# Attention's first casts of k on VectorE, a later clear of zero rows, and expert 6's row loads ahead of its store

## The chip, the cores and the metric

One NeuronCore of a Trainium2 chip runs the whole program in one launch. The metric is the device time of one execution in microseconds; runs of a kernel are told by their median.

## The reference, cut to what matters

```python
scores = scale * np.matmul(q, k.transpose(0, 1, 3, 2))        # 4 x 12 heads, 448 x 64, causal
attn = softmax(masked scores)
x = np.matmul(attn, v) -> 1792 rows of 768
e_idx = np.argmax(x @ w_gate, axis=1)                          # one expert of 8 for each row
for e in range(E):
    ye = np.maximum(x[mask] @ w1[e], 0.0) @ w2[e]              # mask = e_idx == e
    out[mask] = gate_w[mask, None] * eom[mask, e, None] * ye
h = out @ w_in                                                 # last stage, 768 -> 2048 -> 768
return (h - np.tanh(h)) @ w_out
```

## The kernel before, in words

All numbers that TensorE multiplies are kept as two f16 planes, a cast and the rest that the cast left, so almost every load is followed by a cast and a subtraction on some engine. Each engine has one queue of instructions in program order, and SP's queue issues nearly all DMAs.

**Attention** (lines 240 to 760) runs over 24 units of two heads; four heads (two units) share one load, numbered z. For z = 0 the loads come head by head (L285 for q and k, L287 for v), and `kq_part(h)` makes the planes of head h: ScalarE casts q into `qa` (L290), k is cast into `kh` by VectorE for heads 0 and 1 (L292) and by ScalarE for heads 2 and 3 (L294), VectorE subtracts to make `kl` (L295), GpSimd subtracts to make the second half of `qa` (L296). Heads 0 and 1 are done ahead of the loop over units, heads 2 and 3 as parts at the places `START = ((0, 1), (0, 2), ...)` inside unit 0, and v's planes follow (L300 on VectorE, L269 and L270 on GpSimd). For z = 1 and later the casts and rests go to GpSimd and ScalarE (L316, L318, L334), and small DMAs carry the results into `kh`, `qa` and `kl` (L332, L333, L335, L336). The lower 64 partitions of `kl` are filled by those DMAs; the upper 64 must be zero, and GpSimd clears them once for each of the two `kl` tiles: `kls[1]` at L305, between heads 1 and 2 of z = 0, and `kls[0]` at L675, in unit 2. Within a unit, m runs over score tiles: TensorE multiplies (L360, L361), VectorE takes the maximum (L367), ScalarE the exponential (L375).

**Experts.** Each expert has a first slot of 128 rows (expert 0 has two) and up to four extra slots under `If`s on the number of its rows. A slot is two products on TensorE with a relu between (`hh` on ScalarE L171, `hl` on VectorE L172). At the end of a slot `yo` is stored to `ys_d` by SP (L923). In a first slot the next expert's weights are made into planes: `hi(z)` on ScalarE (L115), `lo(z)` on VectorE (L123), and `lo(3)` stands behind the store in the program. For expert 6 `lo(3)` also loads a flag on SP (L1253) and issues six loads of 128 x 768 rows from `ys_d` (`prep0`, L1071) into free parts of the raw weight tiles, for the last stage. In the extra slots `conv_fill` turns three units of the last stage's weights each: SP loads the words into `cu` (L990), VectorE unpacks them into `cc` (L980, L983, L986), ScalarE and VectorE or GpSimd make planes in `co` (L115, L123, L117, L131), and SP stores them to `wb_d` (L1007).

**The last stage** makes planes of the rows in `ys_d`, then 80 tiles of product, activation and product (L1379, L1387 to L1408, L1430) and an indirect store.

What sets the order is the order of the code; each DMA that reads or writes what an earlier DMA touched waits on that DMA's semaphore. In `slot` the end of a slot reads:

```python
        st = nc.sync.dma_start(out=ys_d[ds(r0, 128)], in_=yo).ins      # L923
        ...
        lo(3)
        fill(4)
```

Of the kernel before, what the change touches and what calls it, by code (L numbers as in the profile page):

```python
# [17 lines left out]
AF = mybir.ActivationFunctionType  # L18
# [8 lines left out]
E, F1 = 8, 1024  # L27
# [32 lines left out]
def build(ctx: ExitStack, tc: tile.TileContext, kq0, kq, v, wg, wo, w1, w2, wf, out):  # L60
    nc = tc.nc
# [95 lines left out]
    def slot_xT(src, tag, pool):  # L157
        planes_T(src.rearrange("p (k x n) -> p k x n", k=KD, x=2), xTs[tag][:, 0], xTs[tag][:, 1], pool)
# [22 lines left out]
    with ExitStack() as actx:  # L181
# [68 lines left out]
        def load_32(z):  # L250
            b, hh = divmod(z, 3)
            t32, v32 = views(z)
            nc.sync.dma_start(out=t32, in_=kq[b, hh])
            nc.sync.dma_start(out=v32, in_=v[b, hh])

        kls = [ld.tile([128, HU, S], F16, tag=f"kl{n}", name=f"kl_{n}", bufs=1) for n in range(2)]

        def load_unit(z):
            b, hh = divmod(z, 3)
            t32, v32 = views(z)  # L260
            t = []

            def t_new():
                t.extend((ld.tile([128, HU, S], F16, tag="qa", name=f"qa_{z}"), ld.tile([128, HU, S], F16, tag="kh", name=f"kh_{z}"),
                          kls[z % 2]))

            def v0_planes(hs):
                src = t[3][:, hs, 0, :]
                nc.gpsimd.tensor_scalar(out=t[4][:, 0, hs], in0=src, scalar1=1.0, scalar2=1.0, op0=ALU.mult, op1=ALU.mult)  # L269
                nc.gpsimd.tensor_tensor(out=t[4][:, 1, hs], in0=src, in1=t[4][:, 0, hs], op=ALU.subtract)  # L270

            def v1_new():
                v1 = ld.tile([CP, HU, NCH, D + 1], F32, tag="v1", name=f"v1_{z}", bufs=3)
                nc.gpsimd.memset(v1[:, :, :, D : D + 1], 1.0)
                t.append(v1)
                t.append(ld.tile([CP, 2, HU, D + 1], F16, tag="v0", name=f"v0_{z}", bufs=3))

            if z == 0:
                t_new()
                v1_new()  # L280
                qa, kh, kl = t[0:3]
                f32 = raw2.rearrange("p a b -> p (a b)")[:, 0 : 2 * NS].rearrange("p (h x n) -> p h x n", h=HU, x=2)
                k32, q32 = f32[:, :, 0], f32[:, :, 1]
                for h in range(HU):
                    nc.sync.dma_start(out=f32[:, h : h + 1], in_=kq0[:, h : h + 1])  # L285
                    if h % 2:
                        nc.sync.dma_start(out=v32[:, h - 1 : h + 1], in_=v[b, hh, :, h - 1 : h + 1])  # L287

                def kq_part(h):
                    nc.scalar.activation(out=qa[:, h], in_=q32[:, h], func=AF.Copy)  # L290
                    if h < 2:
                        nc.vector.tensor_copy(out=kh[:, h], in_=k32[:, h])  # L292
                    else:
                        nc.scalar.activation(out=kh[:, h], in_=k32[:, h], func=AF.Copy)  # L294
                    nc.vector.tensor_tensor(out=kl[:, h], in0=k32[:, h], in1=kh[:, h], op=ALU.subtract)  # L295
                    nc.gpsimd.tensor_tensor(out=qa[64:128, h], in0=q32[64:128, h], in1=qa[64:128, h], op=ALU.subtract)  # L296

                def v_part(h):
                    hs = slice(h, h + 2)
                    nc.vector.tensor_scalar(out=t[3][:, hs, :, 0:D], in0=v32[:, hs], scalar1=XS, scalar2=None, op0=ALU.mult)  # L300
                    v0_planes(hs)

                kq_part(0)
                kq_part(1)
                nc.gpsimd.memset(kls[1][64:128], 0.0)  # L305
                return t, (lambda: kq_part(2), lambda: kq_part(3), lambda: v_part(0), lambda: v_part(2))
            if z != 2:
                load_32(z)
            tmp = []

            def cast(y, eng):
                hs = slice(2 * y, 2 * y + 2)
                if y == 0:
                    tmp.extend(ld.tile([128, HU, S], F16, tag=tag, name=f"{tag}_{z}", bufs=1) for tag in ("t16", "lo"))
                if eng == "a":
                    nc.scalar.activation(out=tmp[0][:, hs], in_=t32[:, hs], func=AF.Copy)  # L316
                else:
                    nc.gpsimd.tensor_scalar(out=tmp[0][:, hs], in0=t32[:, hs], scalar1=1.0, scalar2=1.0, op0=ALU.mult, op1=ALU.mult)  # L318

            def rest(y):  # L320
                hs = slice(2 * y, 2 * y + 2)
                if y == 0:
                    t_new()
                    v1_new()
                if z == 1:
                    cast(y, "pa"[y])
                t16, lo = tmp
                qa, kh, kl = t[0:3]
                if z == 1 or y == 0:
                    cs = hs if z == 1 else slice(0, HU)  # L330
                    for p0 in (0, 64):
                        nc.sync.dma_start(out=kh[p0 : p0 + 64, cs], in_=t16[0:64, cs])  # L332
                    nc.sync.dma_start(out=qa[0:64, cs], in_=t16[64:128, cs])  # L333
                nc.gpsimd.tensor_tensor(out=lo[:, hs], in0=t32[:, hs], in1=t16[:, hs], op=ALU.subtract)  # L334
                nc.sync.dma_start(out=qa[64:128, hs], in_=lo[64:128, hs])  # L335
                nc.sync.dma_start(out=kl[0:64, hs], in_=lo[0:64, hs])  # L336
                nc.gpsimd.tensor_scalar(out=t[3][:, hs, :, 0:D], in0=v32[:, hs], scalar1=XS, scalar2=1.0, op0=ALU.mult, op1=ALU.mult)
                v0_planes(hs)

            return t, rest, cast  # L340
# [286 lines left out]
        def fill0(n):  # L627
            for _ in range(n):
                next(s0, None)

        loads = {0: load_unit(0)}
        nc.sync.dma_start(out=wgf[:, :, 0:E], in_=wg)
        nc.sync.dma_start(out=wgf[:, :, E:], in_=wo)
# [18 lines left out]
        for u in range(NU + 5):  # L652
# [18 lines left out]
            for m in range(6):  # L671
                if (u, m) == (0, 3):
                    load_32(2)
                if (u, m) == (2, 0):
                    nc.gpsimd.memset(kls[0][64:128], 0.0)  # L675
                for x, part in zip(START, loads[0][1]):
# [202 lines left out]
    def slot(e, i, w, tag, fill=None, trans=(), then=(), late=False, mid=None):  # L879
        hi, lo = fill if isinstance(fill, tuple) else (lambda z: None, lambda z: None)  # L880
        fill = fill if late else (lambda z: None)
        hh = mt.tile([128, KF1, 128], F16, tag="hh", name=f"hh_{nc.get_next_instruction_name()}", bufs=1)
        hl = mt.tile([128, KF1, 128], F16, tag="hl", name=f"hl_{nc.get_next_instruction_name()}", bufs=1)
        static = isinstance(i, int) and i <= FB[e]
        yo = mt.tile([128, DM], F32, tag="ys" if static else "yo", name=f"yo_{nc.get_next_instruction_name()}", bufs=1)
        trans = list(trans)

        def rows_T(z):
            if trans:
                src, dst = trans.pop(0)  # L890
                slot_xT(rows[src], dst, mp_t)
                if z < len(then):
                    then[z]()

        def out_z(z, py):
            nc.scalar.activation(out=yo[:, z * 384 : (z + 1) * 384], in_=py[:, 0:384], func=AF.Copy)
            fill(2 + z)

        hi(0)
        slot_relu(0, slot_mm1(e, i, 0, w, tag), hh, hl)  # L900
        hi(1)
        lo(0)
        fill(0)
        slot_relu(1, slot_mm1(e, i, 1, w, tag), hh, hl)
        rows_T(0)
        fill(1)
        hi(2)
        lo(1)
        py = slot_mm2(e, i, 0, w, hh, hl, mid)
        hi(3)  # L910
        out_z(0, py)
        rows_T(1)
        lo(2)
        py = slot_mm2(e, i, 1, w, hh, hl)
        hi(4)
        out_z(1, py)
        j = i - FB[e]
        if isinstance(j, int) and j == 0:
            cstr[0] = nc.values_load(cst0[0:1, e : e + 1], engines=(SP,), min_val=0, max_val=NT)
            r0 = cstr[0]  # L920
        else:
            r0 = nc.snap(cstr[0] + j * 128, engines=(SP,), min_val=0, max_val=NT)
        st = nc.sync.dma_start(out=ys_d[ds(r0, 128)], in_=yo).ins  # L923
        if isinstance(i, int):
            tc.declare_no_dep(st, group=f"ys{e}", reason="blocks of one expert have rows of their own in ys_d")
            tc.add_to_no_dep_group(f"ys{e}", st)
            if j == 0 and e:
                after(st, ystores[e - 1])
            ystores.setdefault(e, []).append(st.name)
        lo(3)  # L930
        fill(4)

    cstr = [None]
# [607 lines left out]
```

## Time and profile before

| what | value |
|---|---|
| runs | 998.45, 1002.32, 1003.99 us, median 1002.32 us |
| profiled execution | 1004.1 us, its span 1002.4 us, granted clock 0.994 |
| TensorE busy | 957.7 us (96%) |
| VectorE busy | 787.3 us (79%) |
| ScalarE busy | 615.1 us (61%) |
| GpSimd busy | 471.1 us (47%) |
| DMA | 166.36 MB, mean 166 GB/s |

The page shows the shares over the whole span; the parts of the kernel have different limits, so a stretch is read by its own busy times, its DMA share and the waits of TensorE in it. Times in rows count from the start of the span.

### The profile page before, as it was taken

To read this page: it belongs to the slowest core of one execution; us is meant where nothing else is said; L and a number is where in the kernel's file an instruction comes from. 1 tells how busy PE (TensorE), PEld (TensorE's weight loads), DVE (VectorE), ACT (ScalarE), POOL (GpSimd) and SP (SyncE) were. 2 spreads that over 40 slices of the span, in tenths; PEclk is the share of its full clock that TensorE was granted. 3 is DMA by queue.
4 is the path that set the end of the run, shared out by engine and by line. 5 is a ranking of instruction groups with operands and counts; after the bars stand their busy time and mean duration, and the time that the engine had idled before them with its cause. 6 is when DMAs were issued, how large, how long until landed. Compare 5 with 4: busy or idle time off the path is not lost. (4 is left out here: it accounts for less than half of the span.)

```text
span 1002.4 us, 24099 instructions
## 1 busy us (share of the span) xinstructions
PE 957.7 (96%) x9177; PEld 714.8 (71%) x9177; DVE 787.3 (79%) x1740; ACT 615.1 (61%) x1176; POOL 471.1 (47%) x536
## 2 busy tenths in 40 slices
PE   4999999998999999899999899999999999999996
PEld 3998989986787878667776556666666666667764
DVE  6788888977879598687888999986988788786640
ACT  5898988773645475563346896665655555565530
POOL 8568887872201020201345797564534444453321
PEclk9999999999999999999999999999999999999999
DMA  9787786576799998879877430010000000000000
GB/s 244 204 236 209 226 227 181 162 250 226 261 362 327 383 340 307 327 285 346 320 271 274 169 153 17 32 33 9 32 25 33 17 25 17 9 17 17 16 25 24
DMA packets 59831, 166.36 MB, mean 166 GB/s; under 512 B 7920, under 2 KB 21872, under 8 KB 56608
## 3 DMA queue, kind: packets, MB, share of 16 engines
q1 hardware_dynamic: 55120, 144.68, 43.1%
q0 software_dynamic: 4560, 19.80, 5.7%
q8 instruction: 80, 1.31, 0.5%
q14 instruction: 71, 0.58, 0.2%
HBM read 122.21 MB, written 29.62 MB: 151 GB/s over the span
## 5 line engine op out<-in xcount | busy, mean ns | idle before, releaser
L1430 PE MATMUL fo<-wo,g 128*128 128x384 f16 x1344 | 228.2, 326 | 0.0
L1379 PEld LDWEIGHTS <-raw 128*128 128x128 f16 x1440 | 140.6, 98 | 83.2 <-issue 4.8
L1430 PEld LDWEIGHTS <-g 128*128 128x128 f16 x1344 | 131.1, 98 | 83.9
L1389 POOL TENSOR_TENSOR V<-cu,cc 128x384 f32<-128x384 f32 (+1 forms) x80 | 78.6, 983 | 186.2 <-ACT cu L1388 185.2
L164 PEld LDWEIGHTS <-w 128*128 128x128 f16 x2592 | 145.8, 98 | 7.9 <-issue 6.8
L1379 PE MATMUL fh<-cu,raw 128*128 128x384 f16 (+1 forms) x864 | 131.5, 308 | 2.2 <-DVE cc L1387 2.2
L375 ACT ACTIVATE P<-s,nb 112x112 f32<-112x112 f32 (+1 forms) x192 | 91.2, 508 | 20.7 <-DVE nb L367 18.7
L115 ACT ACTIVATE w<-raw 128x768 f16<-128x768 f32 (+2 forms) x106 | 90.8, 907 | 17.9 <-DMA raw<-w 15.3
L123 DVE SCALAR_TENSOR_TENSOR w<-raw,w 128x768 f16<-128x768 f32 (+1 forms) x99 | 99.7, 1067 | 0.2 <-ACT w L115 0.2
L861 POOL DMA_INDIRECT xg<-xs_d,idx x22 | 26.8, 1218 | 155.2 <-DMA xg<-xs_d,idx 23.5
L1388 ACT ACTIVATE cu<-cc 128x384 f32<-128x384 f32 (+1 forms) x80 | 40.0, 501 | 92.9 <-DVE cc L1387 92.9
L367 DVE CUSTOM_DVE_ANT_0 s<-s,maskw 112x112 f32<-112x112 f32 (+1 forms) x192 | 86.2, 454 | 12.8 <-PE s L361 8.6
L1387 DVE TENSOR_TENSOR cc<-fh,co 128x384 f32<-128x384 f32 (+1 forms) x80 | 42.0, 524 | 63.2 <-PE fh L1379 50.2
L1392 POOL TENSOR_TENSOR X<-cc,X 128x384 f32<-128x384 f32 (+1 forms) x80 | 88.4, 1105 | 4.1 <-ACT X L1391 0.6
L424 PE MATMUL o<-v,PT 112*112 112x65 f32 x576 | 84.5, 270 | 0.0
L1399 DVE SCALAR_TENSOR_TENSOR V<-cu,V 128x384 f32<-128x384 f32 (+1 forms) x80 | 82.3, 1028 | 0.2
L1407 DVE TENSOR_TENSOR V<-V,co 128x384 f32<-128x384 f32 (+1 forms) x64 | 77.8, 1215 | 0.0
L1408 ACT ACTIVATE g<-V 128x384 f16<-128x384 f32 (+1 forms) x80 | 40.0, 500 | 46.2 <-DVE V L1407 46.1
L424 PEld LDWEIGHTS o<-v,PT 112*112 112x112 f32 x576 | 68.4, 179 | 0.0
L1379 PE MATMUL fh<-yh,raw 128*128 128x384 f16 x384 | 67.6, 326 | 0.7 <-DVE cc L1387 0.7
L394 PE MATMUL t<-ident,P 112*112 112x112 f32 x480 | 67.4, 263 | 0.0
L360 PE MATMUL s<-kh,qa 128*112 128x112 f16 (+1 forms) x192 | 53.7, 300 | 13.3 <-POOL qa L296 7.2
(677 smaller groups left out, 2093.9 us busy)
## 6 DMA issues: line engine op xcount, KB each, us to landing
raw<-w SPq DMA_DIRECT2D x48, 512.0 KB, 7.3
raw<-w SPq DMA_DIRECT2D x64, 384.0 KB, 9.4
cu<-wf SPq DMA_DIRECT2D x22, 1024.0 KB, 7.8
wb_d<-co SPq DMA_DIRECT2D x22, 512.0 KB, 7.4
raw<-kq SPq DMA_DIRECT2D x11, 896.0 KB, 7.1
raw<-wb_d SPq DMA_DIRECT2D x8, 768.0 KB, 4.5
xs_d<-xq SPq DMA_DIRECT2D x24, 224.0 KB, 2.3
raw<-v SPq DMA_DIRECT2D x11, 448.0 KB, 7.6
```

What stands on the lines that cost most here:

```text
L115: nc.scalar.activation(out=out, in_=in_, func=AF.Copy, scale=WS)
L123: nc.vector.scalar_tensor_tensor(out=out, in0=in_, scalar=WS, in1=hi, op0=ALU.mult, op1=ALU.subtract)
L164: nc.tensor.matmul(out=ph[:, (f % 4) * 128 : (f % 4 + 1) * 128], lhsT=w[0][:, ww, k, f * 128 : (f + 1) * 128], rhs=xTs[tag][:, xx, k, :], ...
L367: nc.vector.tensor_tensor_reduce(out=d["s", m][:, z, :], in0=d["s", m][:, z, :], in1=maskw[:, S - n : S], scale=-0.125, scalar=3.0e38, op0 ...
L375: nc.scalar.activation(out=d["P"][:, j, OFF[i] : OFF[i] + n], in_=d["s", m][:, z, :], func=AF.Exp, bias=d["nb"][:, 2 * i + j : 2 * i + j + ...
L424: nc.tensor.matmul(out=po[:, i, :], lhsT=d["PT"][:, PT_AT[g], o : o + CP], rhs=d["t"][3][:, hl, j, :], start=(j == 0), stop=(j == i))
L1379: nc.tensor.matmul(out=ph[:, 0:nt], lhsT=wi[ww][:, f // 4, k, f % 4 * 128 : (f % 4 + 1) * 128], rhs=yy[:, k, 0:nt], start=(q == 0), stop=( ...
L1389: nc.gpsimd.tensor_tensor(out=d["V"], in0=d["U"], in1=d["h"], op=ALU.mult)
L1392: nc.gpsimd.tensor_tensor(out=d["X"], in0=d["h"], in1=d["X"], op=ALU.subtract)
L1399: nc.vector.scalar_tensor_tensor(out=d["V"], in0=d[f"S{z}"], scalar=QD[z - 1], in1=d["V"], op0=ALU.add, op1=ALU.mult)
L1407: nc.vector.tensor_tensor(out=d["V"], in0=d["V"], in1=rs_y(g, nt), op=ALU.mult)
L1430: nc.tensor.matmul(out=po[:, 0:384], lhsT=t[:, x, k, i * 128 : (i + 1) * 128], rhs=wo_[ww][:, k, z * 384 : (z + 1) * 384], start=(k == 0 a ...
```

## The change

Heads 2 and 3 of the first load have their k cast by VectorE like heads 0 and 1. The clear of `kls[1]` moves from behind head 1 to the place (0, 3) of the loop over units, behind the parts of heads 2 and 3. In expert 6's first slot `lo(3)`, with the flag's load and the six row loads, is written ahead of the store of the slot's rows; in all other slots it stays behind. Lines of the changed file stand 3 or 4 lower up to L900 and 1 lower at the store (L922 for L923).

```diff
                 def kq_part(h):
                     nc.scalar.activation(out=qa[:, h], in_=q32[:, h], func=AF.Copy)
-                    if h < 2:
-                        nc.vector.tensor_copy(out=kh[:, h], in_=k32[:, h])
-                    else:
-                        nc.scalar.activation(out=kh[:, h], in_=k32[:, h], func=AF.Copy)
+                    nc.vector.tensor_copy(out=kh[:, h], in_=k32[:, h])
...
                 kq_part(0)
                 kq_part(1)
-                nc.gpsimd.memset(kls[1][64:128], 0.0)
...
                 if (u, m) == (0, 3):
                     load_32(2)
+                    nc.gpsimd.memset(kls[1][64:128], 0.0)
...
         out_z(1, py)
+        if e == E - 2:
+            lo(3)
...
-        lo(3)
+        if e != E - 2:
+            lo(3)
         fill(4)
```

On GpSimd, in the first unit (`qa` is q's tile, `kl_175` the cleared one, `v_0_181` v's planes), before and with the change:

```order
-L296 TENSOR_TENSOR qa_177<-raw_90,qa_177 64x448 x2
-L305 MEMSET kl_175 64x1792
-L296 TENSOR_TENSOR qa_177<-raw_90,qa_177 64x448 x2
+L293 TENSOR_TENSOR qa_177<-raw_90,qa_177 64x448 x4
+L670 MEMSET kl_175 64x1792
 L269 TENSOR_SCALAR v_0_181<-v_0_179 112x130
```

The clear now stands behind all four subtractions and directly ahead of v's planes.

On SP, from the end of expert 6's first slot to the first word load of its first extra slot, before (`raw_89`, `raw_90` are the tiles that take the rows, `flg` the flag, `cst` the row offset):

```order
L919 TENSOR_LOAD cst_82
L923 DMA ys_d<-yo_I-16038_16039 128x768 [waits DMAHW3_49,DMAHW4_49,DMAHW2_49,DMAHW6_49,DMAHW1_49,Activation_49]
L1253 TENSOR_LOAD flg
L1071 DMA raw_89<-ys_d 128x768 [waits DMAHW2_49,DVE_49]
L1071 DMA raw_90<-ys_d 128x768 [waits DMAHW0_49]
L949 COMPARE_AND_BRANCH
L990 DMA cu_4988<-wf 128x2048 [waits DMAHW1_49,DVE_49]
```

and with the change:

```order
L1253 TENSOR_LOAD flg
L1071 DMA raw_89<-ys_d 128x768 [waits DMAHW3_49,DMAHW4_49,DMAHW2_49,DMAHW6_49,DMAHW1_49,DVE_49]
L1071 DMA raw_90<-ys_d 128x768 [waits DMAHW7_49]
L918 TENSOR_LOAD cst_82
L922 DMA ys_d<-yo_I-16038_16039 128x768 [waits DMAHW4_49,DMAHW5_49,DMAHW3_49,DMAHW6_49,DMAHW2_49,DMAHW7_49,DMAHW0_49,Activation_49]
L949 COMPARE_AND_BRANCH
L990 DMA cu_4988<-wf 128x2048 [waits DMAHW1_49,DVE_49]
```

Four of the six loads and register instructions are left out of both. Before, the first load waits on the store's semaphore; with the change the store waits on the loads' semaphores, and the branch and the word load stay behind whichever is last.

## Rows read from the trace of the kernel before

**Rows 1.** Busy us by stretch, PE to POOL (instructions), then clock, DMA share, GB/s.

```profile
10.00:15.00 5.00, 2.90 (x11) 1.53 (x11) 4.96 (x15) 3.31 (x7) 2.60 (x7) 1.00 1.05 275
...
30.00:60.00 30.00, 30.00 (x380) 28.76 (x379) 24.76 (x101) 26.15 (x57) 17.45 (x24) 1.00 0.76 208
...
440.00:445.00 5.00, 5.00 (x80) 4.55 (x78) 4.22 (x6) 3.66 (x6) 0.74 (x1) 1.00 0.22 83
...
460.00:465.00 5.00, 2.79 (x22) 1.53 (x20) 3.76 (x7) 2.91 (x5) 3.91 (x4) 1.00 1.01 379
...
600.00:1000.00 400.00, 394.23 (x2586) 248.50 (x2583) 294.38 (x500) 218.19 (x445) 180.94 (x173) 1.00 0.06 22
```

**Rows 2.** Timeline, VectorE, first unit: start us, us, engine, line, operation, idle before.

```profile
4.47 0.39 DVE L292 CAST kh<-raw 128x448 f16<-128x448 f32 x1 [1.32 <-DMA raw<-kq]
...
5.78 0.88 DVE L292 CAST kh<-raw 128x448 f16<-128x448 f32 x1 [0.26 <-DMA raw<-kq]
...
9.47 1.10 DVE L295 TENSOR_TENSOR kl<-raw,kh 128x448 f16<-128x448 f32 x1 [0.38 <-ACT kh L294]
...
11.31 1.09 DVE L295 TENSOR_TENSOR kl<-raw,kh 128x448 f16<-128x448 f32 x1
```

**Rows 3.** Timeline, GpSimd, first unit and the start of the second load's casts.

```profile
7.50 1.59 POOL L305 MEMSET kl<- 64x1792 f16 x1
...
10.89 1.03 POOL L296 TENSOR_TENSOR qa<-raw,qa 64x448 f16<-64x448 f32 x1 [0.80 <-ACT qa L290]
13.35 0.32 POOL L269 TENSOR_SCALAR v<-v 112x130 f16<-112x130 f32 x1 [1.43 <-DVE v L300]
...
15.42 0.99 POOL L318 TENSOR_SCALAR t<-raw 128x896 f16<-128x896 f32 x1 [0.40 <-DMA raw<-kq]
```

**Rows 4.** Timeline, TensorE and VectorE, where unit 2 begins.

```profile
24.18 0.23 PE L360 MATMUL s<-kh,qa 128*112 128x112 f16 x1 [2.83 <-DMA qa<-lo]
...
24.85 0.28 DVE L367 CUSTOM_DVE_ANT_0 s<-s,maskw 112x112 f32<-112x112 f32 x1 [1.82 <-PE s L361]
```

**Rows 5.** DMA issue of q's piece at 17.7 us, with us from issue to landing.

```profile
qa<-t SPq DMA_DIRECT2D x1, 112.0 KB, 6.2
```

**Rows 6.** Timeline of SP's queue around the end of expert 6's first slot.

```profile
442.63 0.35 SPq L923 DMA_DIRECT2D ys_d<-yo_I-16038_16039  x1
445.32 3.28 SPq L1071 DMA_DIRECT2D raw<-ys_d  x6
449.69 0.34 SPq L990 DMA_DIRECT2D cu<-wf  x1
```

**Rows 7.** Landing of the last weight load before them, issued at 432.4.

```profile
raw<-w SPq DMA_DIRECT2D x1, 384.0 KB, 8.4
```

**Rows 8.** SP's instructions at the skipped branch (L949) and for the flag (L1253).

```profile
L949 SPq EVENT_SEMAPHORE  x9: 17/17/17, 438.0 to 441.2; - x9
...
L1253 SPq TENSOR_LOAD <-flg x1: 282/282/282, 443.0 to 443.0; - x1
...
L1253 SPq SEQ_ASSERT  x1: 18/18/18, 443.6 to 443.6; - x1
```

**Rows 9.** Landings: store at 442.63, last row load (448.2), word load at 449.69.

```profile
ys_d<-yo_I-16038_16039 SPq DMA_DIRECT2D x1, 384.0 KB, 2.6
...
raw<-ys_d SPq DMA_DIRECT2D x2, 384.0 KB, 6.7
...
cu<-wf SPq DMA_DIRECT2D x1, 1024.0 KB, 8.3
```

**Rows 10.** Landing of the word load at 275.4, issued to an idle DMA.

```profile
cu<-wf SPq DMA_DIRECT2D x1, 1024.0 KB, 5.0
```

**Rows 11.** Timeline, VectorE, ScalarE, TensorE: the wait in the second extra slot.

```profile
458.06 0.76 DVE L980 TENSOR_SCALAR cc<-cu 128x512 uint32<-128x512 uint32 x2 [3.98 <-DMA cu<-wf]
...
461.85 0.58 ACT L171 ACTIVATE hh_I-16751_16752<-ph_I-16757_16758 128x512 f16<-128x512 f32 x1
...
462.49 0.50 PE L176 MATMUL py_I-16960_16961<-w,hh_I-16751_16752 128*128 128x384 f16 x2 [1.99 <-ACT hh_I-16751_16752 L171]
```

## Prediction

> **What bounds the kernel now.** I read the busy times by stretch first, because the two edits lie far apart and the shares over the whole span mix stages. Three things are to be seen in [rows 1]. From 600 us on, and from 30 to 60 us, TensorE is busy nearly throughout, so what happens ahead reaches the end only as a later or earlier start. At 10 to 15 us TensorE works 2.90 of 5 us while the DMA share is full. At 460 to 465 us it works 2.79 of 5. So each edit has one question: does it move the point at which TensorE becomes busy again? For that I read the timelines at both places, then the landings of DMAs and SP's queue.
>
> The front first. Unit 2's first product starts at 24.18 us after an idle of 2.83 us that a DMA ends [rows 4]. q's piece for it was issued at 17.7 and took 6.2 us to land [rows 5], hence 23.9: it stood among the full DMA traffic of the first loads. That traffic, not VectorE, sets the start of unit 2; VectorE itself stands idle for 1.82 us before its first maximum there [rows 4].
>
> Then expert 6. In its second extra slot TensorE waits 1.99 us for `hh` [rows 11]. The chain runs backwards: the relu on ScalarE (461.85) stands behind the planes of the third weight unit; those need VectorE's unpacking, which begins at 458.06 after 3.98 us of idle, when the words loaded into `cu` have landed [rows 11]. That load was issued at 449.69 and took 8.3 us [rows 6, 9]. Ahead of it on SP stand the store at 442.63 and the six row loads, which could start at 445.32 only, because the store took 2.6 us to land [rows 6, 9]. This is the one place where the second edit can touch TensorE.
>
> **The first edit, part by part.** Two casts leave ScalarE for VectorE. One cast takes 0.39 us, or 0.88 beside a subtraction on GpSimd [rows 2]. For head 2 VectorE had stood idle 0.38 us for ScalarE's cast [rows 2], so it loses 0.01 to 0.50; for head 3 it did not wait, so it loses 0.39 to 0.88. The clear of 1.59 us moves from 7.50 to behind the fourth subtraction, which ends at 11.92 [rows 3], and so lies beside head 3's `kl` instead of head 1's. VectorE's `kl` took 1.09 and 1.10 us beside subtractions already [rows 2], so I count this at nothing, with half a microsecond either way. Together VectorE runs late by 0 to 1.9 us; I take 0.8, two casts at 0.39 to 0.88 less the 0.38 of idle. GpSimd then starts v's planes at about 14.15 instead of 13.35 and has 0.40 us of idle ahead of 15.42 [rows 3], so its cast for the second load is late by 0.4.
>
> None of it should reach the end. VectorE's lateness has the 1.82 us of idle ahead of 24.85 to vanish in [rows 4]; 0.8 fits, and if that cover were gone each further tenth would count in full. The pieces issued 0.4 late still join the same traffic, for which the DMA share is 1.05 [rows 1]. ScalarE's freed time is worth nothing, as nothing waits for it after 24.18. A gain is excluded because the bytes ahead of q's piece stay the same. Term: 0, between 0 and 2.0 (all of the lateness, if the traffic hid none).
>
> The Trainium skill, SBUF — State Buffer, section Who interferes with whom, says that a cast in VectorE's two-port mode and a GpSimd instruction exclude each other for the whole instruction. The rows lean that way: 5.78 plus 0.88 ends close behind a GpSimd subtraction. By this rule the lateness lies at the top of my range, since head 3's cast could stand behind the whole clear.
>
> **The second edit, part by part.** No instruction and no byte is added. VectorE's order stays, since the store is SP's. SP's order changes: flag, six loads, store, branch, word load.
>
> When can the loads start? SP is held at the branch that expert 5 skipped until 441.2 [rows 8], because there it waits for the last weight load, issued at 432.4 and 8.4 us on its way [rows 7]. Behind it come some register work and the flag, 443.0 to 443.6 before [rows 8], so the first load goes at about 442.3: 3.0 us earlier than 445.32. VectorE's readers of the raw tiles no longer hold it then. The DMAs are nearly idle there (share 0.22 from 440 to 445 [rows 1]), so these 3 us are real.
>
> Now the new wait. The store waits for all six loads, because it writes the tensor that they read. The last goes out 2.9 us after the first, at 445.2. Its landing took 6.7 us with other traffic behind it [rows 9]; I take 6.2, so 451.4 (450.2 to 451.9, by 5.0 to 6.7, the lower end being a larger load to an idle DMA [rows 10]). Behind the store SP needs 0.35 for its issue [rows 6], then the branch and a table read, 1.09 between the end of the loads at 448.60 and the word load at 449.69 [rows 6]. So the word load goes out at 451.4 + 1.45 = 452.85, against 449.69: 3.2 us **later**. But it finds a DMA with only the store ahead of it. The nearest row for that is the word load at 275.4, 5.0 us to land [rows 10], against 8.3 here [rows 9]. It lands at 457.85, VectorE starts at 457.9 instead of 458.06, and TensorE's wait shrinks by 0.2 us.
>
> Bounds: earliest 450.2 + 1.45 + 5.0 = 456.65, a gain of 1.4; latest 451.9 + 1.45 + 8.3 = 461.65, a loss of 3.6. I take the 5.0 because it is the only landing to an idle DMA. Queued behind the waiting store are also the first unit's store to `wb_d` and the second word load; the latter would go out near 455.3 and is read after 464, so 5.0 to 8.3 us of landing fit. The slot's output buffer is not written again before expert 7. Past 462 the slots follow each other on TensorE, so what is won or lost there is carried to 600 and the end.
>
> The Trainium skill, DMA: Bandwidth & Descriptors, section Queues, rings and completion order, says that each DMA engine takes descriptors of one ring in order. By it the traffic behind the word load does not delay it, the 8.3 us were due to the row loads ahead, and the sum is -0.2; if landings of 7 us and more had come from traffic behind, the sum would be a loss, as in case B.
>
> **Sum**: 0 - 0.2 = -0.2 us. The profiled execution took 1004.1 us (1002.4 of it span) and would take 1003.9; it lies 1.8 above the median of the runs, 1002.32, so the forecast for the median is 1002.1.
>
> **The rivals.**
> - A, the forecast: the later issue and the shorter landing cancel within a microsecond. 1002.1; chance 0.55.
> - B, SP's queue becomes the limit: the store holds the word load back, and it still takes 7.0 to 8.3 us, as under load. VectorE starts at 459.85 to 461.15, TensorE loses 1.8 to 3.1. For it: 8.3 in [rows 9]. Against it: the idle DMA. It decides from a landing of 5.2 us on, since 452.85 + 5.2 reaches 458.06. 1004.1 to 1005.4, slower; chance 0.2.
> - C, the loads land fast on idle DMAs: first at 442.3 + 2.6 (the store's landing [rows 9]), then 1.0 us each (384 KB at the 379 GB/s of a full DMA [rows 1]), the last at 449.9; word load at 451.35, landed in 4.3 (2.6 and 640 KB more at that rate) to 5.0. VectorE starts at 455.7 to 456.4 and 1.7 to 2.0 of the wait go. 1000.3 to 1000.6; chance 0.15.
> - D, the front slides: head 3's cast waits until the clear ends at 13.5, VectorE is 2.0 late, more than its 1.82 of idle. Between 0.2 (what passes the idle) and 2.0: 1002.5 to 1004.3; chance 0.1.
>
> **How the numbers follow.** The cases span 1000.3 to 1005.4. The three runs lie 5.5 us apart, so a median moves by about 1.7 either way without cause. The range is 998.6 to 1005.8. A measurement of this kernel can tell about 0.5%, 5 us. No case reaches that by itself: faster needs under 997.3, slower over 1007.3, and only a mechanism that I don't see, or the spread on top of B or C, gives either. Faster 0.04, same 0.92, slower 0.04.
>
> **What would show it.** In the changed profile: the first row load near 442.3; the store on SP near 451.4, held by the loads' landing; the word load near 452.85, landing in about 5 us; VectorE's unpacking near 457.9 and TensorE's wait near 1.8 us. At the front: unit 2's first product still near 24.2, VectorE's idle ahead of it shorter by about 0.8. Wrong is the forecast if the row loads start well before 442 (SP not held at the branch), if the store does not wait for them, or if unit 2 starts over 0.5 us later.

## The result and the profile after

The changed kernel takes 1006.0 us (median of 22 runs, 1001.03 to 1011.05) where the kernel before, run beside it, takes 1000.53 us (22 runs, 996.34 to 1007.09). The ratio is 1.0054 with an interval of [1.0039, 1.007]: **slower by 0.54%, 5.4 us**, where the forecast was no change and rival B, slower by 1.8 to 3.1 us, had a chance of 0.2.

The two profiled executions do not show this difference: 1004.41 us after (span 1002.7) against 1004.1 before (span 1002.4). The first is 1.6 us below its median, the second 3.6 above its own. So a pair of traces shows the mechanism here and not the size, and the traces of the experiments are read along with them.

What answers to [rows 1], busy time by stretch of the changed kernel:

```profile
10.00:15.00 5.00, 1.54 (x4) 0.69 (x4) 4.90 (x12) 1.59 (x4) 2.70 (x2) 1.00 0.98 306
...
440.00:445.00 5.00, 5.00 (x44) 3.32 (x42) 4.08 (x8) 1.72 (x3) 0.94 (x1) 1.00 0.95 324
445.00:450.00 5.00, 5.00 (x49) 3.58 (x48) 4.81 (x10) 2.14 (x5) 0.00 (x0) 1.00 0.49 197
450.00:455.00 5.00, 5.00 (x94) 5.00 (x91) 1.17 (x3) 0.66 (x2) 0.00 (x0) 1.00 0.94 307
455.00:460.00 5.00, 2.93 (x46) 2.37 (x43) 3.53 (x7) 2.20 (x5) 2.33 (x3) 1.00 1.00 360
...
600.00:1000.00 400.00, 394.52 (x2587) 248.89 (x2585) 293.66 (x501) 218.58 (x446) 179.88 (x172) 1.00 0.06 22
```

From 600 us on nothing changed. From 440 to 445 the DMAs work at once (share 0.95 for 0.22), which is what the earlier row loads buy. From 445 to 450 they fall to half: that is the price, as SP's queue shows, the answer to [rows 6]:

```profile
437.21 3.12 SPq L1071 DMA_DIRECT2D raw<-ys_d  x6
447.86 0.35 SPq L922 DMA_DIRECT2D ys_d<-yo_I-16038_16039  x1
449.46 0.34 SPq L990 DMA_DIRECT2D cu<-wf  x1
450.59 0.66 SPq L1007 DMA_DIRECT2D wb_d<-co  x1
```

```profile
SPq L922 <- DMA raw<-ys_d: 6.6, 4, 2.6
```

The second fence is the waits of SP (us in total, times, longest). SP stood 6.6 us at the store for the six row loads; the store left 7.9 us after the last of them (440.0), and from 446.5 to 448.5 almost no byte moved (51 GB/s in the first of these us, 0 in the second). The word load for the third unit of the first extra slot came behind it. The row loads themselves could start when SP was done with the skipped branch, at 435.9 (SP's instructions at that line, first and last start):

```profile
L949 SPq EVENT_SEMAPHORE  x9: 17/17/17, 433.5 to 435.9; - x9
```

The two traces don't stand at the same time here: the first product of expert 6's first extra slot begins at 435.12 before and at 432.05 after (timelines of TensorE, before and after), so what follows is counted from there.

```profile
435.12 4.18 PE L164 MATMUL ph_I-16407_16408<-xT,w 128*128 128x128 f16 x72
```

```profile
432.05 4.18 PE L164 MATMUL ph_I-16407_16408<-xT,w 128*128 128x128 f16 x72
```

The wait in the second extra slot, the answer to [rows 11], in the timelines of VectorE, ScalarE and TensorE:

```profile
454.83 0.76 DVE L980 TENSOR_SCALAR cc<-cu 128x512 uint32<-128x512 uint32 x2 [3.83 <-DMA cu<-wf]
...
457.80 1.15 ACT L115 ACTIVATE co<-cc 128x512 f16<-128x512 f32 x2 [7.14 <-DMA wb_d<-co]
458.86 0.58 ACT L171 ACTIVATE hh_I-16751_16752<-ph_I-16757_16758 128x512 f16<-128x512 f32 x1
...
459.49 0.50 PE L176 MATMUL py_I-16960_16961<-w,hh_I-16751_16752 128*128 128x384 f16 x2 [2.06 <-ACT hh_I-16751_16752 L171]
```

TensorE waits 2.06 us where it waited 1.99. In this execution VectorE began to unpack 22.8 us after the first product of the first extra slot, where it began 22.9 us after it in the kernel before. What ended last for ScalarE is a second thing that stood behind the held store: the unit's store to `wb_d` (450.59), which frees the planes' buffer `co`.

The front, the answer to [rows 2 to 4] (timelines of VectorE, GpSimd, TensorE):

```profile
9.10 1.05 DVE L291 CAST kh<-raw 128x448 f16<-128x448 f32 x1
...
11.52 1.95 DVE L291 CAST kh<-raw 128x448 f16<-128x448 f32 x1
...
14.05 0.51 DVE L363 CUSTOM_DVE_ANT_0 s<-s,maskw 112x336 f32<-112x336 f32 x1
...
11.64 1.59 POOL L670 MEMSET kl<- 64x1792 f16 x1
...
24.52 0.27 PE L356 MATMUL s<-kh,qa 128*112 128x112 f16 x1
```

Head 3's cast took 1.95 us beside the clear, and VectorE's next maximum began at 14.05 instead of 12.33 (timeline before):

```profile
12.33 0.50 DVE L367 CUSTOM_DVE_ANT_0 s<-s,maskw 112x336 f32<-112x336 f32 x1
```

Unit 2 began at 24.52 instead of 24.18, but without an idle of 2.83 us ahead of it.

### The profile page after: what moved, and what is told of

Same layout as the page of the kernel before. It is cut to its first block, busy times and chain, and to the rows that moved or that the text cites. A ratio compares the mean times of both kernels' runs of the same rounds, so it can differ in the third digit from the quotient of the medians.

```text
span 1002.7 us, 24096 instructions
## 1 busy us (share of the span) xinstructions
PE 959.2 (96%) x9177; PEld 715.9 (71%) x9177; DVE 790.1 (79%) x1742; ACT 613.9 (61%) x1174; POOL 471.6 (47%) x536
## 5 line engine op out<-in xcount | busy, mean ns | idle before, releaser
L1392 POOL TENSOR_TENSOR X<-cc,X 128x384 f32<-128x384 f32 (+1 forms) x80 | 91.7, 1146 | 4.1 <-ACT X L1391 0.5
```

What stands on the lines that cost most here:

```text
L1392: nc.gpsimd.tensor_tensor(out=d["X"], in0=d["h"], in1=d["X"], op=ALU.subtract)
```

## The experiments

Each experiment ran 12 times beside 23 to 35 runs of the kernel before. The table gives the ratio on record with its 95% interval (it isn't the quotient of the medians that the text gives), and from the trace three times in us of TensorE and SP: how long after the first product of expert 6's first extra slot the first word load left SP; how long TensorE then waited in the second extra slot, and for what (hh is the relu's result, xg the gathered rows); and the time from expert 6's first product to the start of the last output half of expert 7's extra slot.

| kernel | ratio to before | word load out | wait | experts 6 and 7 |
|---|---|---|---|---|
| before | | 14.57 | hh 2.0 | 121.8 |
| the change | 1.0054 [1.0039, 1.007] | 17.41 | hh 2.1 | 122.3 |
| the change again | 1.0053 [1.0027, 1.008] | 18.50 | hh 3.3 | 124.2 |
| expert 6's edit alone | 1.0037 [1.0011, 1.0062] | 19.82 | hh 6.9 | 124.1 |
| both front edits | 1.0009 [0.9982, 1.0036] | 15.39 | hh 2.5 | 119.9 |
| casts alone | 1.0007 [0.9984, 1.003] | 15.49 | hh 2.4 | 118.1 |
| clear alone | 1.0017 [0.9991, 1.0044] | 14.92 | hh 1.9 | 118.5 |
| store on GpSimd's queue | 0.9995 [0.9969, 1.0022] | 13.29 | xg 2.7 | 118.2 |
| loads of other rows | 0.9994 [0.9974, 1.0014] | 13.85 | hh 2.0 | 119.6 |
| loads on GpSimd's queue | 1.0017 [0.9991, 1.0042] | 13.12 | xg 1.1, hh 1.1 | 119.7 |
| loads late | 1.0008 [0.998, 1.0035] | 13.12 | none | 124.3 |
| loads in the slot | 1.001 [0.9989, 1.0031] | 13.13 | hh 3.3 | 123.8 |

The last column has to be read with care. Expert 6's first slot lies ahead of the edit, and TensorE spent 18.2 to 23.3 us in it in these traces. Without that slot the column reads 98.7 for the kernel before; 100.5, 100.9 and 104.8 for the three traces with a held store; 103.5 and 102.3 for the loads late and in the slot; and 98.7 to 100.5 for the other six.

**Which edit?** The front's two edits together, expert 6's edit alone, the casts alone and the clear alone; these are the lines, in the order casts, clear, expert 6, of which each kernel has its part:

```diff
+                    nc.vector.tensor_copy(out=kh[:, h], in_=k32[:, h])
...
+                    nc.gpsimd.memset(kls[1][64:128], 0.0)
...
+        if e == E - 2:
+            lo(3)
```

> The two edits of the front alone: both late casts of k on VectorE and the later clear, expert 6 as before. If the loss of 5.4 us sits in expert 6, this is no slower than before, or 0 to 1.5 us faster, since in the traced run of the change unit 2 ran at full clock and the front was 1.35 us ahead. If the loss sits in the front (VectorE late by 1.6 us in unit 0), it is slower by 4 to 6 us.

> Only expert 6's row loads ahead of its store, the front as before. If the loss sits in expert 6, slower by 4 to 7 us; if it sits in the front, within 1 us of before, as forecast (-0.2).

> Only the two casts of k on VectorE; the clear stays between heads 1 and 2. The third cast no longer runs beside the clear (1.95 us there in the changed kernel), so VectorE should be late by 0.5 to 0.9 instead of 1.6. If the loss is the front's lateness, about half of it or less shows here (0 to 3 us slower); if expert 6's, no more than 1 us either way.

> Only the later clear of the zero rows; casts as before. If the front matters through VectorE's lateness, this is within 1 us of before, since the clear then lies beside a subtraction that ran at 1.09 us anyway. A loss of several us would say that the clear's place by itself counts, through GpSimd's planes of v and the casts for the second load.

The front's edits measured 1002.1, 1000.69 and 1001.17 us, none apart from the kernel before (1001.43). Expert 6's edit alone measured 1003.17 and is slower, by 3.7 us at its ratio and by 1.7 between the medians, under the 4 to 7 us that were expected. So this run says where the loss sits and leaves its size open; that the front has no part in it that shows is settled by the two experiments below that keep the front's edits and show no loss. The trace of expert 6's edit shows the mechanism at its dearest:

```profile
434.99 4.14 SPq L1074 DMA_DIRECT2D raw<-ys_d  x6
446.43 0.36 SPq L925 DMA_DIRECT2D ys_d<-yo_I-16038_16039  x1
448.02 0.34 SPq L993 DMA_DIRECT2D cu<-wf  x1
```

```profile
456.02 0.76 DVE L983 TENSOR_SCALAR cc<-cu 128x512 uint32<-128x512 uint32 x2 [8.86 <-DMA cu<-wf]
```

```profile
455.00:460.00 5.00, 0.00 (x0) 0.00 (x0) 3.17 (x6) 1.33 (x3) 1.24 (x2) 0.82 0.89 306
460.00:465.00 5.00, 4.55 (x15) 1.93 (x16) 4.57 (x8) 1.58 (x3) 3.71 (x4) 0.50 0.82 288
```

The word load took 8.0 us to reach VectorE. The last view is busy time by stretch: TensorE did nothing from 455 to 460, and when it resumed at 460.45 its granted clock was 0.50, the 1.2 GHz level. The first output half took 6.2 us where it takes 3.9 at 2.4 GHz, so here a wait of 6.9 us cost 2.3 us more than its length. Behind the changed kernel's wait of 2.1 us the clock stayed at 1.00.

**The change once more**, beside the experiments:

> The changed kernel once more, for a second trace and more runs. Theory S (the store waits for the six row loads and holds the word load behind it on SP): the store stands on SP for about 6.5 us behind the last row load's issue, the word load goes out at or behind the start of slot 2's first product (it was 1 to 2 us ahead of it in kernels without the edit), and TensorE's wait ahead of slot 2's second product is between 2 and 7 us, where kernels without the edit show 2.0 to 2.7. Median 3 to 6 us above before. Theory N (the traced wait of 2.2 in the changed kernel is typical and the time is lost elsewhere): wait 2.2 again.

1006.09 against 1000.37: the loss is there again. The words were unpacked 5.7 us after their load left (451.76 to 457.49), TensorE waited 3.3 us, and the clock gave way behind it:

```profile
460.00:465.00 5.00, 2.85 (x13) 1.33 (x14) 3.76 (x8) 2.91 (x5) 4.45 (x5) 0.86 0.99 381
465.00:470.00 5.00, 5.00 (x26) 2.76 (x25) 4.64 (x9) 1.64 (x3) 0.51 (x1) 0.80 0.76 254
```

**Take the store out of SP's queue.** The changed kernel, where this one store goes out on GpSimd's queue (its row offset read there too); it still has to wait for the row loads, but nothing of SP stands behind it.

```diff
-        st = nc.sync.dma_start(out=ys_d[ds(r0, 128)], in_=yo).ins
+        st = (nc.gpsimd if isinstance(j, int) and j == 0 and e == E - 2 else nc.sync).dma_start(out=ys_d[ds(r0, 128)], in_=yo).ins
```

> The change, but the store of expert 6's first slot is issued on GpSimd's queue, so that its wait for the row loads no longer stands ahead of the word load on SP. Theory S: the word load goes out some 5 us earlier, TensorE's wait in slot 2 falls to 0 to 2 us, and the kernel is back at the time of before or up to 2 us faster. Theory D (the row loads' traffic on the DMAs, not the queue, makes the word load late): the wait stays at 2 to 7 us and the kernel 3 to 5 us slower than before.

999.66 us: the whole loss is gone.

```profile
435.72 4.13 SPq L1072 DMA_DIRECT2D raw<-ys_d  x6
441.55 0.34 SPq L991 DMA_DIRECT2D cu<-wf  x1
```

```profile
446.12 0.62 POOL L923 DMA_DIRECT2D ys_d<-yo_I-16038_16039  x1 [25.99 <-ACT co L115]
447.10 1.01 POOL L858 DMA_INDIRECT xg<-xs_d,idx  x1 [0.36 <-issue]
```

The word load leaves early, but the store now holds GpSimd's queue, and the gather of rows behind it came 2.7 us late for TensorE. (The view puts the store's idle of 25.99 us down to ScalarE's work on `co`, which the store doesn't read; the store left 6.6 us after the last row load.) The wait moved, so it is no gain over the kernel before.

**Take the wait away and leave all else.** The changed kernel, whose row loads read as many bytes of another DRAM tensor, so that the store has nothing to wait for (the last stage then gets other rows, and the result is not the reference's).

```diff
-        src = ys_d[bk * 128 : (bk + 1) * 128] if r0 is None else ys_d[ds(r0, 128)]
+        src = ys_d[bk * 128 : (bk + 1) * 128] if r0 is None else xs_d[ds(r0, 128)].bitcast(F32)
```

> The changed kernel, whose six early row loads read the same number of bytes from the same offsets of attention's output in DRAM instead of the tensor that the store writes (so the last stage's first blocks are not the reference's): the same order on SP and the same traffic, but the store has nothing to wait for. Theory (the loss is the store's wait for the six landings, with the word load queued behind it): the store follows the last row load's issue by the register read, the word load 1 to 2 us later, 3 us or more ahead of the second extra slot's first product; 999 to 1001.5 where before is 1000.5, ratio 0.999 to 1.001, the loss of 0.5% gone. Rival (the six loads' traffic, started 3 to 8 us earlier, is what costs): 1004 to 1006.5, ratio 1.003 to 1.006, as the change itself.

1000.75 us against 1001.16: the loss is gone again, with the same order on SP and the same early traffic.

```profile
437.54 4.20 SPq L1071 DMA_DIRECT2D raw<-xs_d  x6
442.60 0.35 SPq L922 DMA_DIRECT2D ys_d<-yo_I-16038_16039  x1
444.05 0.34 SPq L990 DMA_DIRECT2D cu<-wf  x1
```

```profile
453.14 0.76 DVE L980 TENSOR_SCALAR cc<-cu 128x512 uint32<-128x512 uint32 x2 [3.99 <-DMA cu<-wf]
```

The store followed the end of the loads' issue by 0.9 us instead of 7.5. The expectation of an early word load held only in part: it left 2.7 us ahead of the second extra slot's first product, not 3, and, with the six loads and the store ahead of it, took 9.1 us to reach VectorE. TensorE waited 2.0 us as in the kernel before. So early loads as such neither cost nor gain here; the store's wait costs. Both experiments keep the front's edits, so these cost nothing that shows either.

**Other places for the row loads.** If their landing stands in the way of the words, another place may beat both kernels. Three were tried on the kernel before: at the start of expert 7; on GpSimd's queue behind the store; and in expert 6's first extra slot, directly behind the first word load (and in an `Else`, for when that slot is skipped). The first takes the five lines from `fill_lo` to the head of expert 7's block, the second replaces the queue, and the third has:

```diff
                     conv_load(cu[b], unit_of(e, n0 + j + min(c, 2)))
+                    if e == E - 2 and i == 1 + FB[e] and z == 1:
+                        early_rows()
```

> The kernel before with the six row loads moved out of expert 6's first slot to the start of expert 7, ahead of its first slot. Both theories: the word load has neither store nor row loads ahead of it, lands by about 452, and the 2.0 to 2.7 us of TensorE's wait in slot 2 go. 2 us faster than before, if the maxima over the rows at expert 7 do not wait for the loads (landing within 8 us of the issue suffices); by up to 3 us slower if they do.

> The kernel before (store first) with the six row loads and their flag on GpSimd's queue. Theory S: SP goes from the store to the word load at once, some 5 us earlier than before; GpSimd waits for the store's landing instead, where it is idle. TensorE's wait in slot 2 shrinks, 1 to 2 us faster than before. Theory D: the row loads share the DMAs with the word load in either queue, so the word load lands no earlier and the time is that of before.

> The kernel before, with the six row loads and their flag taken out of expert 6's first slot and issued inside its first extra slot, directly behind the first word load (and in an Else branch when that slot is skipped). Theory (what counts is how early the first word load leaves SP's queue against TensorE): nothing of the row loads stands ahead of the first word load, so it goes out at the skipped branch's end plus the store's issue, 3 us or more ahead of the second extra slot's first product (1.94 ahead in the trace of before), lands in 5 to 6 us, and the waits of VectorE and TensorE in the second extra slot go. Price: the second and third word loads stand behind the row loads, but they are read a slot later. 997.5 to 1000 where before is 1000.5, ratio 0.997 to 0.9995. Rival (the 2.3 MB of row loads cost the same wherever they are put, since the words then come late in the third piece): 1000.5 to 1003, with a wait of 2 us or more for cu at the second or third unit.

They measured 1001.77, 1002.08 and 1002.6 us, none apart from the kernel before (1000.37, 1000.37, 1001.16). Each took the row loads from ahead of the word load and made a new wait. Late loads, at expert 7's start (waits of VectorE):

```profile
DVE wo L1081 <- DMA raw<-ys_d: 5.4, 2, 4.3
```

On GpSimd's queue they held the gather (waits of TensorE):

```profile
PE pt_I-16909_16910 L151 <- DMA xg<-xs_d,idx: 1.1, 1, 1.1
PE py_I-16960_16961 L176 <- ACT hh_I-16751_16752 L171: 1.1, 1, 1.1
```

In the slot, the words were there in time (load at 445.18, unpacked from 450.93 without a wait), but the unit's store, issued behind the row loads, freed `co` late (timelines of SP and ScalarE):

```profile
445.18 0.35 SPq L993 DMA_DIRECT2D cu<-wf  x1
446.22 3.02 SPq L1085 DMA_DIRECT2D raw<-ys_d  x6
450.03 0.66 SPq L1010 DMA_DIRECT2D wb_d<-co  x1
...
459.02 1.15 ACT L115 ACTIVATE co<-cc 128x512 f16<-128x512 f32 x2 [8.35 <-DMA wb_d<-co]
```

Where these expectations look for a gain, they missed: whatever stands behind 2.3 MB of row loads is late in its turn, first the words, then the buffer that the unit's store frees. No version tried beats the kernel before.

## Why the prediction was wrong, by its own steps

**The front, term 0.** Right that none of it reaches the end, but the cover that it named was that of one execution. VectorE ran 1.7 us late in the first unit, at the top of the range of 0 to 1.9, where 0.8 was taken, and GpSimd's cast for the second load 1.3 us (16.69 for 15.42), where 0.4 was. The rule of the Trainium skill, SBUF — State Buffer, section Who interferes with whom, was the better guide to that: the 1.95 us cast covers the clear of 11.64 to 13.23. (The page gives the shared ports to whichever is issued first; by the rows the cast began 0.12 us ahead of the clear, and yet the cast was the long one.) The start of unit 2 that the traffic was said to set, 24.18 behind an idle of 2.83 us [rows 4], was a late one. The four other traces with the front as before begin unit 2 at 22.93 to 23.34, three of them behind such an idle, of 1.1 to 1.6 us. This is the row from expert 6's edit alone (timeline of TensorE):

```profile
22.93 0.23 PE L360 MATMUL s<-kh,qa 128*112 128x112 f16 x1 [1.15 <-DMA qa<-lo]
```

The five with both front edits begin it at 23.95 to 24.52 without that idle, 0.9 us later on average. Yet nothing of it is left at expert 6's first product, at 410.2 us on average in both groups, and the three front runs show no loss. Behind its long idle the kernel before ran at a granted clock down to 0.50 (its busy time by stretch):

```profile
24.00:26.00 2.00, 1.81 (x18) 1.78 (x19) 0.68 (x4) 0.87 (x3) 0.95 (x2) 0.75 0.90 202
26.00:28.00 2.00, 2.00 (x15) 1.97 (x13) 0.76 (x3) 0.88 (x4) 0.00 (x0) 0.50 0.89 326
```

Its way to expert 6's first product was the longest of all traces, 412.1 us against 408.3 to 410.6. The changed kernel's trace is 1.8 us ahead there, loses 0.5 by expert 7's extra slot and 1.6 in the last stage: that is why the pair of traces shows so little.

**When the row loads start.** Right by its mechanism: SP was done with the branch at 435.9, and the first load left 1.3 us later (1.1 forecast). But the branch ended earlier than the kernel before had it: the first load left 5.2 us after the first product of the extra slot, where 7.2 follow from the forecast (442.3 less 435.12).

**How long the store waits.** Mis-sized, beyond its bounds. 6.2 us from the last load's issue (5.0 to 6.7) were taken; 7.9, 8.0 and 7.6 were measured in the three traces with a held store. The upper bound was the same load's landing in the kernel before; why it is a microsecond more here, no run tells.

**When the word load leaves.** 17.7 us after the first product of the extra slot were forecast. 17.4 was measured in the changed kernel's trace, 18.5 and 19.8 in the other two: the forecast was near once, and up to 2.1 too early. The near hit is luck, since loads that left 2.0 us earlier and a wait that was 1.7 longer cancelled.

**How long it takes: this is the step that failed.** "I take the 5.0 because it is the only landing to an idle DMA." Until the unpacking it was 5.4, 5.7 and 8.0 us in the three traces. The rival named 5.2 as the point from which it decides, so all lie on B's side of it. Against the forecast, the unpacking was late by 0.8 us of later departure and 0.7 of longer landing in the second trace of the change, and by 2.1 and 3.0 in that of expert 6's edit alone. So the two terms that were to cancel did not: behind the held store the load left later than forecast, and its landing was not as short. The forecast was right that the load finds a DMA with little ahead of it: by the packets in the traces, its first packet of 8 KB started 1.0 us after the issue in all three, and 3.5 in the kernel before. The Trainium skill, DMA: Bandwidth & Descriptors, section Queues, rings and completion order, says that each DMA engine takes the descriptors of one ring in order; the forecast drew from it that traffic behind a load doesn't delay it, which is near to the 5.4 and 5.7. It doesn't explain the 8.0: ahead of that load stood the same single store as in the other two. The packets say where the time went: the 122nd of the load's 128 had started 4.0, 4.1 and 4.3 us after the issue, so in the dear trace, too, the bulk of the load was quick, and its last few packets, it seems, kept the reader waiting.

**What else was queued.** The forecast named the first unit's store to `wb_d` behind the held store, and asked only whether the words come in time. ScalarE needs that store's landing too, to write `co` again: it ended last in the changed kernel's trace and in the slot experiment.

**The price.** The chain was right as far as the forecast followed it: in the changed kernel's own trace VectorE began 22.8 us after the slot's first product, as forecast (by the same luck), and TensorE waited 2.1 us, where about 1.8 were forecast. But that trace is a cheap case; 3.3 and 6.9 us are the others. And no step counted the clock. Each run's mean granted clock is on record. Over 34 runs of the change it is 0.9918 on average, over 93 of the kernel before 0.9940; within either kernel a run is 0.76 to 0.80 us longer for each 0.001 less. So of the 5.0 us between the means (1006.2 and 1001.2), about 1.7 (0.0022 by 0.78 per 0.001) go with the clock, and 3.3 are left at equal clock. That is a little over B's price of 1.8 to 3.1; the rest goes with a lower clock. That the longer waits lowered it is argued from the two traces above and not shown for the runs, since no experiment held the clock fixed.

**The baseline and the range.** The median of three runs was 1.8 above the one of 22. The forecast range, 998.6 to 1005.8, ends 0.2 below the measured median; 0.92 for no change rested on the belief that B cannot reach 5 us.

What stays open: why the last packets of the word load came late once. In the three traces with a held word load, and in three of the other eight (both front edits, other rows, loads on GpSimd's queue), the time from the last output half of expert 7's extra slot to the end is 1.3 us or more above the kernel before's 468.55; the last section shows what goes with it, and whether the edit makes it likelier was not tried.

## What to carry to other kernels

When a DMA is moved ahead of another on one in-order queue, ask whether the second must wait for the landing of the first: a store that waits for loads holds all that is issued behind it, and here 3 us of earlier loads cost 6.6 us of a standing queue. Count everything behind the wait, also the stores that free a buffer, and price a wait of TensorE above its length, because the clock may be lower when it resumes. Where runs of one kernel differ by more than the effect looked for, a pair of traces gives the mechanism, and only many runs give its size.

## What the runs showed of the hardware

Behind the same wait the clock falls in some executions only. In the last stage TensorE waits 2.04 us for `yh` in both kernels' traces, and the 18 products behind it took 3.09 us before and 4.77 after (timelines of TensorE, before and after):

```profile
568.36 3.09 PE L1379 MATMUL fh<-cu,raw 128*128 128x384 f16 x18
```

```profile
567.29 4.77 PE L1379 MATMUL fh<-cu,raw 128*128 128x384 f16 x18
```

Busy by stretch, before and after: TensorE's busy time in the stretch is nearly the same, the granted clock is 1.00 in one and 0.74 in the other.

```profile
565.00:570.00 5.00, 2.96 (x27) 1.89 (x25) 4.49 (x9) 4.96 (x13) 2.71 (x4) 1.00 0.24 59
```

```profile
565.00:570.00 5.00, 3.04 (x15) 1.65 (x15) 4.50 (x8) 4.97 (x13) 2.71 (x4) 0.74 0.31 70
```

All that follows is 1.6 us later (from the last output half of expert 7's extra slot to the end 468.55 us before, 470.15 after). The other five traces with a long tail have a drop there too, to between 0.69 and 0.75 in one stretch of 5 us; the other six, the kernel before among them, read 1.00 there. The run-to-run spread of one kernel goes with its clock: the 93 runs of the kernel before average 999.4 us where the mean granted clock is 0.995 or more (33 runs), and 1005.7 where it is 0.990 or less (5 runs).
